# Three small operations per attention unit move from GpSimd to VectorE in six steps of a fused attention and MoE kernel

## The chip, the cores and the metric

One core of a Trainium2 chip runs the kernel. The metric is the device time of one execution in microseconds. Engines are named as in the profile: PE (TensorE; PEld its weight loads), DVE (VectorE), ACT (ScalarE), POOL (GpSimd), SP (SyncE, which issues DMAs).

## The reference

Three layers, one behind the other, all in float32:

```python
def _attn_ref(q, k, v):          # 4 x 8 heads, 576 tokens, head_dim 64
    scores = scale * np.matmul(q, k.transpose(0, 1, 3, 2))
    kth = np.partition(scores, -top_k, axis=-1)[..., -top_k:-top_k + 1]   # top_k = 32
    scores = np.where(scores >= kth, scores, -1000000000.0)
    attn = np.exp(scores - np.max(scores, axis=-1, keepdims=True))
    attn = attn / (np.sum(attn, axis=-1, keepdims=True) + 1e-09)
    return np.matmul(attn, v)

def _moe_ref(x, w_in, w_out):    # x: 2304 x 512, w_in: 512 x 2048, w_out: 2048 x 512
    h = x @ w_in
    g = h * np.clip(h + 3.0, 0.0, 6.0) / 6.0
    return g @ w_out
```

The third layer routes each token to one of 8 experts (512 x 1024 and 1024 x 512) and scales the expert's output by a gate.

## The kernel before, in words

The attention is cut into 72 units, of 128 query rows of two heads each (or the same amount of remaining rows). A loop of 76 steps runs them as a software pipeline: in step i the scores of unit i are made, unit i-1 is searched for its 32 largest scores, unit i-2 is masked, unit i-3 is exponentiated and divided by its sum, unit i-4 is transposed, and every second step two units are multiplied with the values. Between these a step does one eighth of a group of the second layer (`s10`, `s11`, `gate`, `swish`, `large`, `small`, `s20`, `s21`), and up to step 18 it prepares that layer's weights, two pieces a step (`one`, `two`, `round`, `add`, `hi`, `low`, `store`). The routed experts follow from about 700 us on.

The order of the work is written out by hand: the string `FIRST` for steps 0 to 11, `MID` for steps 12 to 20 (`MOES` is 12, `WORDS` 21), `THEN` and `ODD` after that. Each word of the string issues one part, and the engines execute their instructions in that order; there is no other scheduler. What the change and the prediction speak of:

- `pick0` to `pick3` (L474, L477; DVE): four rounds of the search, two MAX8 each, the first three followed by match-and-replace; the last pair has 576 elements a row. `A` holds the 32 values.
- `bounds` (L482, L484; POOL): `nb`, from the largest and the 32nd value, the bias of the exponential and of the mask; and `viol`, differences of the selected values that are looked at once at the end, as a guard on the selection. Both are 128x4.
- `bend` (L488; ACT) and `mask` (L492; POOL): the mask of the next step, from `nb`.
- `expo` (L498; ACT): exponential with the sum of each row in `sums` (128x2).
- `guard` (L502; POOL): adds 1e-9 to `sums`. `inverse` (L505; DVE): reciprocal of it. `scale` (L512 on ACT for units below 16, L514 on POOL after that): multiplies the unit with it.
- `turn` (L525; PE): transposes of the scaled unit, in the next step, and `keep` (L530; ACT), their copy out of PSUM.
- `pairs` (L455 to L459; DVE): five operations that order the scores of the newest unit for the search. `swish` (L619; DVE), `xl` (L575; DVE, behind ACT's `xh`, L560), `small` (L626; POOL, behind ACT's `large`, L623).
- The weights: `one` (L241), `two` (L248) on DVE, `round` (L256) and `hi` (L269) on ACT, `add` (L261, behind `two` and `round`) and `low` (L273, behind `hi`) on POOL. There are 32 pieces; steps 12 to 16 do `one` and `two` for two each, step 17 for the last one.

In `MID` DVE's order is `one0 two0 pick0 one1 pick1 two1 pick2 inverse swish pick3 xl pairs`, and POOL's is `lows low0 guard low1 add0 mask0 add1 mask1 bounds small`.

Of the kernel before, what the change touches and what calls it, by code (L numbers as in the profile page):

```python
# [14 lines left out]
ALU = mybir.AluOpType  # L15
# [8 lines left out]
TOPK = 32  # L24
# [18 lines left out]
RAMP, MOES, WORDS = 3, 12, 21  # L43
FIRST = ("hi0 s10 expo0 lows hi1 turn0 one0 s11 s20 low0 round0 two0 ship keep0 turn1 expo1 guard bend0 keep1 add0 turn2 load0 "
         "store0 one1 load_k inverse keep2 prep mask0 pick0 round1 score0 gate take0 scale two1 bend1 load_q swish large values xh "
         "score1 pick1 pick2 aside s21 add1 load1 xl pick3 need_v low1 take1 store1 pairs mask1 bounds small")
MID = ("lows turn0 hi0 turn1 low0 s10 s11 ship keep0 one0 keep1 expo0 two0 pick0 load_k turn2 store0 one1 pick1 expo1 hi1 guard "
       "round0 bend0 two1 score0 pick2 keep2 low1 s20 take0 gate bend1 inverse add0 score1 values take1 round1 scale swish mask0 "
       "large s21 add1 xh pick3 need_v prep xl mask1 load_q bounds small store1 load0 load1 pairs aside")
THEN = ("lows pick0 turn0 expo0 keep0 ship expo1 pick1 bend0 s10 guard turn1 place pick2 inverse score0 mask0 turn2 s11 take0 "  # L50
        "keep1 bend1 pick3 need_v gate load_k score1 swish keep2 scale aside load_q bounds values take1 mask1 xh large xl prep "
# [47 lines left out]
def layers(tc: tile.TileContext, qt, kt, v, w_in, w_out, embt, tau, w1, w2, out, y_dram, yq_dram, g_dram, tbl, xq_dram, lo_dram, flag, pools, consts):  # L99
    nc = tc.nc  # L100
# [20 lines left out]
    viol = const.tile([128, NUNIT, 2, 2], BF16, name="viol")  # L121
    kb = const.tile([128, 2, 2], F32, name="kb")
# [187 lines left out]
    sel, pts, sums = {}, {}, {}  # L310
# [168 lines left out]
    def bounds(i):  # L479

        A, nb = sel[i]
        nc.gpsimd.tensor_tensor(nb, A[:, :, 0:TOPK:TOPK - 1], kb, op=ALU.mult)  # L482
        if not exact:
            nc.gpsimd.tensor_tensor(viol[:, i, :, :], A[:, :, TOPK - 1:TOPK].broadcast_to([128, 2, 2]), A[:, :, 15:24:8], op=ALU.subtract)  # L484

    def relu(i, n):

# [11 lines left out]

    def guard(i):  # L500
        sel.pop(i)
        nc.gpsimd.tensor_scalar(sums[i], sums[i], 1e-9, None, op0=ALU.add)  # L502

    def inverse(i):
        nc.vector.reciprocal(sums[i], sums[i])  # L505
# [375 lines left out]
    def step(i, last):  # L881
# [15 lines left out]
        def after(o):  # L897
            if last:
# [3 lines left out]
                   s10=lambda: part(a, 1, 0), s11=lambda: part(a, 1, 1), gate=lambda: lows() if i in (1, 2) else part(a, 2), swish=lambda: part(a, 3), large=lambda: part(a, 4), small=lambda: part(a, 5),  # L902
                   s20=lambda: after(0), s21=lambda: after(1), aside=aside, place=place,
                   guard=lambda: at_(3, guard), inverse=lambda: at_(3, inverse), scale=lambda: at_(3, scale), bounds=lambda: at_(1, bounds),
                   pairs=lambda: at_(0, pairs), values=lambda: both(values), xh=lambda: both(finish), xl=lambda: both(finish_low))
        for name, j, f, n in (("bend", 2, relu, 2), ("mask", 2, mask, 2), ("expo", 3, expo, 2), ("pick", 1, select, 4),
# [3 lines left out]
        def pair(f, j, c):  # L910
            n = pair_of(i - j, c)
            if n >= 0:
                f(n)
        for name, f, j in (("load", w_load, -1), ("one", w_one, 0), ("two", w_two, 0), ("round", w_round, 0), ("add", w_add, 0),
                           ("hi", w_hi, 1), ("low", w_low, 1), ("store", w_store, 1)):
            for c in range(2):
                ops[name + str(c)] = lambda f=f, j=j, c=c: pair(f, j, c)
        names = (FIRST if i < MOES else MID if i < WORDS else ODD if i % 2 else THEN).split()
        if i == 0:
# [480 lines left out]
```

## Time and profile before

| | |
|---|---|
| three runs | 1007.87, 1010.01, 1005.36 us (median 1007.87) |
| the profiled execution, its own time | 1007.83 us |
| its span, first to last instruction | 1005.8 us |
| mean granted clock of PE, share of full speed | 0.969 |
| busy share of the span | PE 93%, DVE 77%, ACT 71%, POOL 63% |

In the profile a group or an instruction stands as line, engine, operation, output<-inputs, output<-input (partitions x elements, type) and its count; the time that an engine was idle before an instruction stands in brackets with what ended it. Times in the trace are microseconds from the start of the span. Steps are told apart by `bounds`, which each step issues once: step 12 ends at about 121, step 13 at 131.5, step 14 at 142, step 15 at 153.3, step 16 at 164.7, step 17 at 175.6.

### The profile page before, as it was taken

The numbers are of one execution on the slowest core, as the hardware profiler recorded it, in microseconds if no ns is written. First come the engines' busy times: TensorE is split into PE (matmuls) and PEld (weight loads), VectorE is DVE, ScalarE is ACT, GpSimd is POOL, SyncE is SP. The second block draws the span as 40 slices with busy tenths as digits, with TensorE's granted clock in tenths as the row PEclk, the third lists the DMA queues.
The fourth block names the chain that finished last, engine by engine and source line by source line (L and its number), as shares of the span: only waits on it lengthen the run. The fifth ranks groups of instructions, "written<-read, shape, count | busy, mean of one in ns | idle before, by whom it ended". The sixth has DMA issues, their size and how long they took to land. (4 is left out here: it accounts for less than half of the span.)

```text
span 1005.8 us, 20687 instructions
## 1 busy us (share of the span) xinstructions
PE 934.8 (93%) x7128; PEld 820.3 (82%) x7128; DVE 778.1 (77%) x2364; ACT 712.8 (71%) x1441; POOL 637.9 (63%) x786
## 2 busy tenths in 40 slices
PE   3656688999999999999999999999999999999997
PEld 1433467989899899998998988889898988999986
DVE  7999999899989989989989899882134354666660
ACT  5899889888889788789778787785335454555551
POOL 5889899677778788688788666665333453134210
PEclk9966799999999999999999999999999999999998
DMA  7655676664456754456665476477586467767730
GB/s 251 211 177 162 213 237 234 207 202 149 141 168 195 249 184 131 137 189 192 221 177 146 143 227 202 139 237 203 172 262 223 133 226 263 242 200 239 255 124 23
DMA packets 100689, 193.21 MB, mean 192 GB/s; under 512 B 16189, under 2 KB 42448, under 8 KB 100575
## 3 DMA queue, kind: packets, MB, share of 16 engines
q1 hardware_dynamic: 95983, 181.74, 56.3%
q0 software_dynamic: 4448, 10.00, 3.2%
q8 instruction: 58, 0.95, 0.4%
q14 instruction: 56, 0.46, 0.1%
q10 hardware_dynamic: 144, 0.07, 0.0%
HBM read 163.64 MB, written 24.92 MB: 187 GB/s over the span
## 5 line engine op out<-in xcount | busy, mean ns | idle before, releaser
L492 POOL TENSOR_TENSOR s<-s,z 128x576 f32<-128x576 f32 x144 | 191.4, 1330 | 61.6 <-ACT z L488 61.0
L607 PE MATMUL bank_h<-xh,vh 128*128 128x256 f32 x576 | 171.6, 298 | 0.0
L607 PE MATMUL bank_h<-xh,lo 128*128 128x256 f32 x576 | 163.7, 284 | 0.0
L607 PE MATMUL bank_h<-xl,vh 128*128 128x256 f32 x576 | 163.6, 284 | 0.0
L474 DVE MAX8 A<-left 128x8 f32<-128x288 f32 (+1 forms) x288 | 159.5, 594 | 0.0
L525 PE MATMUL bank_t<-both,s 128*128 128x128 f32 x648 | 108.1, 290 | 30.8 <-ACT pt L530 18.1
L525 PEld LDWEIGHTS bank_t<-both,s 128*128 128x128 f32 x648 | 81.2, 148 | 53.2 <-ACT pt L530 24.2
L530 ACT COPY pt<-bank_t 128x384 f32<-128x384 f32 x216 | 101.5, 478 | 26.2 <-PE bank_t L525 26.2
L626 POOL TENSOR_TENSOR gl<-u,gh 128x512 fp32r<-128x512 f32 x72 | 93.1, 1293 | 41.6 <-ACT gh L623 41.5
L642 PE MATMUL y<-wh,gh 128*128 128x512 f32 x288 | 116.5, 405 | 0.0
L488 ACT ACTIVATE z<-s,nb 128x576 bf16<-128x576 f32 x144 | 112.2, 780 | 4.4 <-POOL nb L482 4.3
L446 ACT COPY s<-ps_sc 128x576 f32<-128x576 f32 x143 | 92.3, 645 | 32.5 <-PE ps_sc L439 11.0
L498 ACT ACTIVATE s<-s,nb 128x576 f32<-128x576 f32 x144 | 113.0, 786 | 1.5 <-POOL s L492 1.5
L642 PE MATMUL y<-lo,gh 128*128 128x512 f32 x288 | 113.5, 394 | 0.0
L642 PE MATMUL y<-wh,gl 128*128 128x512 f32 x288 | 113.2, 393 | 0.0
L607 PEld LDWEIGHTS bank_h<-xl,vh 128*128 128x128 f32 x576 | 111.2, 193 | 0.3
L607 PEld LDWEIGHTS bank_h<-xh,vh 128*128 128x128 f32 x576 | 111.1, 193 | 0.3
L607 PEld LDWEIGHTS bank_h<-xh,lo 128*128 128x128 f32 x576 | 110.7, 192 | 0.0
L1038 POOL DMA_INDIRECT out_dram<-ob,idt x21 | 25.8, 1228 | 123.4 <-ACT ob L1031 92.3
L514 POOL TENSOR_SCALAR s<-s,sums 128x576 f32<-128x576 f32 x112 | 82.5, 748 | 20.7 <-DVE sums L505 20.2
L543 PE MATMUL bank_a<-pt,vt 128*64 128x128 f32 (+1 forms) x1600 | 93.7, 275 | 0.9 <-ACT pt L530 0.9
L615 ACT ACTIVATE u<-bank_h,half 128x512 f32<-128x512 f32 x72 | 50.0, 694 | 61.8 <-PE bank_h L607 61.8
(266 smaller groups left out, 2611.6 us busy)
## 6 DMA issues: line engine op xcount, KB each, us to landing
lo<-lo_dram SPq DMA_DIRECT2D x144, 512.0 KB, 4.6
a<-in_moe_w_dram SPq DMA_DIRECT2D x64, 512.0 KB, 6.1
vt<-in_v_dram SPq DMA_DIRECT2D x28, 320.0 KB, 4.4
w<-in_moe_w_in_dram SPq DMA_DIRECT2D x16, 512.0 KB, 3.9
w<-in_moe_w_out_dram SPq DMA_DIRECT2D x16, 512.0 KB, 4.3
lo_dram<-wf SPq DMA_DIRECT2D x32, 256.0 KB, 2.7
qraw<-in_q_dram SPq DMA_DIRECT2D x48, 128.0 KB, 2.9
krs<-in_k_dram SPq DMA_DIRECT2D x16, 288.0 KB, 4.7
```

Source lines behind the costliest of these rows:

```text
L446: nc.scalar.copy(sbuf[i % NS][:, :, HS * g:HS * g + HS], ps_[i][:, :, :HS])
L474: nc.vector.max(A[:, n, 8 * r:8 * r + 8], src[:, n, :w])
L488: nc.scalar.activation(zb_[n], tile_of(i, n), AF.Relu, bias=sel[i][1][:, n, 1:2], scale=-BIG)
L492: nc.gpsimd.tensor_tensor(s, s, zb_[n], op=ALU.subtract)
L498: nc.scalar.activation(s, s, AF.Exp, bias=sel[i][1][:, n, 0:1], scale=SCALE, accum_out=sums[i][:, n:n + 1])
L514: nc.gpsimd.tensor_scalar(x, x, rv[:, n:n + 1], 1.0, op0=ALU.mult, op1=ALU.mult)
L525: nc.tensor.transpose(pp[:, 128 * k:128 * k + 128], e[:, 128 * (3 * c + k):128 * (3 * c + k) + 128], ident)
L530: nc.scalar.copy(pts[i][:, 3 * c:3 * c + 3, :].rearrange("p k n -> p (k n)"), tb_.pop((i, c))[:, :384])
L543: nc.tensor.matmul(av[64 * n:64 * n + 64, c0:c1], vt[:, k, 64 * n:64 * n + 64], pt[:, k + 5 * n if k < 4 else 4, c0:c1], start=(o == 0), s ...
L607: nc.tensor.matmul(ph[:, a, :], w, x[:, k, :], start=(k == 0 and n == 0), stop=(k == 3 and n == 2))
L626: nc.gpsimd.tensor_tensor(state[q][1], state.pop((q, "u")).rearrange("p (a n) -> p a n", a=2), state[q][0].bitcast(F32), op=ALU.subtract)
L642: nc.tensor.matmul(state["y"][o], x[:, a, c], w, start=(f == 0 and n == 0), stop=(f == 15 and n == 2))
```

## The change

In steps 12 to 17 (`MOES <= step < WORDS - 3`) the two operations of `bounds` and the one of `guard` are issued to DVE instead of POOL; the units are those that are in the respective stage in these steps, six for each stage. In `MID` the word `guard` moves from behind `hi1` to just ahead of `inverse`. Elsewhere the three stay on POOL. Nothing else changes: the operations, their shapes and their data are the same.

```diff
-MID = ("... pick1 expo1 hi1 guard "
-       "round0 bend0 two1 score0 pick2 keep2 low1 s20 take0 gate bend1 inverse add0 score1 ..."
+MID = ("... pick1 expo1 hi1 "
+       "round0 bend0 two1 score0 pick2 keep2 low1 s20 take0 gate bend1 guard inverse add0 score1 ..."
...
     def bounds(i):
         A, nb = sel[i]
-        nc.gpsimd.tensor_tensor(nb, A[:, :, 0:TOPK:TOPK - 1], kb, op=ALU.mult)
+        by = nc.vector if MOES <= i + 1 < WORDS - 3 else nc.gpsimd
+        by.tensor_tensor(nb, A[:, :, 0:TOPK:TOPK - 1], kb, op=ALU.mult)
         if not exact:
-            nc.gpsimd.tensor_tensor(viol[:, i, :, :], A[:, :, TOPK - 1:TOPK].broadcast_to([128, 2, 2]), A[:, :, 15:24:8], op=ALU.subtract)
+            by.tensor_tensor(viol[:, i, :, :], A[:, :, TOPK - 1:TOPK].broadcast_to([128, 2, 2]), A[:, :, 15:24:8], op=ALU.subtract)
...
     def guard(i):
         sel.pop(i)
-        nc.gpsimd.tensor_scalar(sums[i], sums[i], 1e-9, None, op0=ALU.add)
+        (nc.vector if MOES <= i + 3 < WORDS - 3 else nc.gpsimd).tensor_scalar(sums[i], sums[i], 1e-9, None, op0=ALU.add)
```

## Rows read from the trace of the kernel before

**Rows 1.** The page, its first part: busy time, share of the span, instructions.
```profile
PE 934.8 (93%) x7128; PEld 820.3 (82%) x7128; DVE 778.1 (77%) x2364; ACT 712.8 (71%) x1441; POOL 637.9 (63%) x786
```
**Rows 2.** Windows of single steps: length, busy time by engine, granted clock, DMA share, GB/s.
```profile
142.00:153.30 11.30, 11.30 (x93) 9.33 (x92) 11.14 (x31) 10.15 (x21) 11.14 (x12) 0.92 0.70 239
153.30:164.70 11.40, 8.95 (x59) 7.49 (x58) 10.99 (x34) 10.44 (x23) 11.13 (x13) 0.98 0.77 265
164.70:175.60 10.90, 10.55 (x86) 9.49 (x86) 9.88 (x30) 10.90 (x24) 10.73 (x12) 0.86 0.54 168
175.60:184.10 8.50, 8.46 (x58) 7.45 (x57) 8.30 (x30) 8.50 (x18) 7.74 (x10) 1.00 0.52 145
```
**Rows 3.** Waits from 110 to 182 us: total us, times, longest.
```profile
PEld bank_t L525 <- ACT s L512: 11.4, 4, 5.4
...
ACT s L512 <- DVE sums L505: 5.3, 5, 2.5
...
DVE xl L575 <- ACT xh L560: 1.9, 3, 0.9
```
**Rows 4.** Timeline of PE, 160 to 215 us: start, duration, instruction, idle before.
```profile
163.52 1.33 PE L525 MATMUL bank_t<-both,s 128*128 128x128 f32 x6 [1.90 <-ACT s L512]
...
176.14 0.82 PE L525 MATMUL bank_t<-both,s 128*128 128x128 f32 x6
```
**Rows 5.** Timeline of DVE, steps 12 to 14.
```profile
118.48 0.15 DVE L505 RECIPROCAL sums<-sums 128x2 f32<-128x2 f32 x1
...
129.10 0.15 DVE L505 RECIPROCAL sums<-sums 128x2 f32<-128x2 f32 x1
...
133.74 0.42 DVE L241 TENSOR_SCALAR wf<-w 128x512 int32<-128x512 int32 x1
134.19 0.69 DVE L248 SCALAR_TENSOR_TENSOR wf<-w,wf 128x512 int32<-128x512 int32 x1
...
139.79 0.15 DVE L505 RECIPROCAL sums<-sums 128x2 f32<-128x2 f32 x1
139.86 0.66 DVE L619 SCALAR_TENSOR_TENSOR u<-u,bank_h 128x512 f32<-128x512 f32 x1
```
**Rows 6.** Groups by line, DVE, 110 to 176: busy us, mean ns, idle before.
```profile
L248 DVE SCALAR_TENSOR_TENSOR wf<-w,wf 128x512 int32<-128x512 int32 x11 | 11.2, 1021 | 0.2
...
L241 DVE TENSOR_SCALAR wf<-w 128x512 int32<-128x512 int32 x11 | 7.2, 658 | 0.0
```
**Rows 7.** Timeline of DVE at 215 and at 704 us.
```profile
215.56 0.70 DVE L182 TENSOR_SCALAR nr<-nr,tb 128x8 f32<-128x8 f32 x1
...
704.98 0.35 DVE L755 TENSOR_TENSOR pos<-pos,picks 128x16 f32<-128x16 f32 x1
```
**Rows 8.** Timeline of POOL at the same places.
```profile
215.50 0.73 POOL L415 TENSOR_TENSOR ql<-qraw,qh 128x256 fp32r<-128x256 f32 x1 [0.69 <-ACT qh L408]
...
704.01 1.28 POOL L626 TENSOR_TENSOR gl<-u,gh 128x512 fp32r<-128x512 f32 x1 [4.37 <-ACT gh L623]
```
**Rows 9.** Timeline of POOL, steps 12 to 14.
```profile
118.44 1.28 POOL L492 TENSOR_TENSOR s<-s,z 128x576 f32<-128x576 f32 x1
...
129.01 1.29 POOL L261 TENSOR_TENSOR wf<-wf,w 128x512 int32<-128x512 int32 x1 [0.27 <-ACT w L256]
...
134.41 0.54 POOL L502 TENSOR_SCALAR sums<-sums 128x2 f32<-128x2 f32 x1 [1.31 <-ACT s L498]
...
139.42 1.29 POOL L261 TENSOR_TENSOR wf<-wf,w 128x512 int32<-128x512 int32 x1
```
**Rows 10.** Groups by line, POOL, 110 to 176 us.
```profile
L502 POOL TENSOR_SCALAR sums<-sums 128x2 f32<-128x2 f32 x6 | 2.0, 342 | 1.7 <-ACT s L498 1.3
...
L482 POOL TENSOR_TENSOR nb<-A,kb 128x4 f32<-128x4 f32 x6 | 1.2, 200 | 0.9 <-DVE A L474 0.9
```
**Rows 11.** Timeline of DVE at 347 us, each reading what the one before wrote.
```profile
347.65 0.17 DVE L736 TENSOR_REDUCE mxs<-l_all 128x4 f32<-128x32 f32 x1
347.86 0.19 DVE L738 TENSOR_TENSOR eqs<-l_all,mxs 128x32 f32<-128x32 f32 x1
```

More of the change, by code (lines that the diff above doesn't have):

```diff
@@ L46 @@
          "score1 pick1 pick2 aside s21 add1 load1 xl pick3 need_v low1 take1 store1 pairs mask1 bounds small")
-MID = ("lows turn0 hi0 turn1 low0 s10 s11 ship keep0 one0 keep1 expo0 two0 pick0 load_k turn2 store0 one1 pick1 expo1 hi1 guard "
-       "round0 bend0 two1 score0 pick2 keep2 low1 s20 take0 gate bend1 inverse add0 score1 values take1 round1 scale swish mask0 "
+MID = ("lows turn0 hi0 turn1 low0 s10 s11 ship keep0 one0 keep1 expo0 two0 pick0 load_k turn2 store0 one1 pick1 expo1 hi1 "
+       "round0 bend0 two1 score0 pick2 keep2 low1 s20 take0 gate bend1 guard inverse add0 score1 values take1 round1 scale swish mask0 "
        "large s21 add1 xh pick3 need_v prep xl mask1 load_q bounds small store1 load0 load1 pairs aside")
```

## The prediction

> **What bounds the kernel now.** I began with the page: over the span TensorE (PE) is busiest, 934.8 us of 1005.8 [rows 1]. That is an average over stages, and the change touches only steps 12 to 17 of the attention loop, 110 to 176 us, so I read the windows of single steps next [rows 2]. In step 14 to 15 (142.0 to 153.3) VectorE (DVE) is busy 11.14 of 11.30 us and GpSimd (POOL) also 11.14; one step on, 10.99 and 11.13 of 11.40, with PE at 8.95. In step 17 to 18 (175.6 to 184.1) PE has 8.46 of 8.50 and POOL falls to 7.74. So two engines are full in the steps that are changed, and PE is full right behind them. Which of the two full ones sets the pace is read from who waits [rows 3]: PE's weight loads waited 11.4 us for ACT's scaling L512, ACT's scaling waited 5.3 us for DVE's inverse L505, DVE itself waited only 1.9 us, for an ACT copy. In this stretch nobody's row names POOL's bounds, differences or guards as what it waited for. The chain is: DVE's queue, inverse, ACT's scale, PE's transposes of the next step. PE last waits on it at 163.52 (1.90 us idle behind L512); the transposes of the step after, at 176.14, start with no wait [rows 4]. So what DVE loses up to the inverse of step 16 goes to the end one for one; what it loses after that meets a PE that is behind anyway.
>
> **What DVE's time holds.** An unhindered L241 took 0.42 us and L248 0.69 (at 133.74 and 134.19) [rows 5]; over steps 12 to 17 the eleven of each have means of 0.658 and 1.021 us [rows 6]. That is 11 x 0.24 + 11 x 0.33 = 6.2 us in which DVE executes nothing but is not idle in the record. What it waits for shows best in two small operations. A TENSOR_SCALAR of 128x8 took 0.70 us, from 215.56 to 216.26, and a TENSOR_TENSOR of 128x16 with both inputs in SBUF 0.35 us, from 704.98 to 705.33 [rows 7]; POOL was inside an operation both times, from 215.50 to 216.23 and from 704.01 to 705.29 [rows 8]. Both ended some 0.03 to 0.04 us behind POOL. The inverse, a reciprocal with one input, took its 0.15 us at 118.48, 129.10 and 139.79 [rows 5] although POOL was inside L492 or L261 each time [rows 9]. So some forms on DVE wait until POOL's running operation is over, and the three that the change brings are of the two forms that waited: the guard is a TENSOR_SCALAR, bounds and differences are TENSOR_TENSORs with two SBUF inputs.
>
> **The change part by part.**
>
> *Leaving POOL.* Per step POOL loses a guard (0.34 us), bounds (0.20) and differences (as long as the bounds) [rows 10]: 0.74 us. I cost this at nothing, since nobody waits for POOL there; if that cover is gone it is a gain, the first rival. No operation that moves issues a DMA, so no queue of SP or POOL changes its order. In steps 18 to 20 the guard stays on POOL and is only written further down the list; on POOL's queue it passes nothing there (the second weight subtraction is empty by then): nothing.
>
> *Issue time on DVE.* Independent small operations start 0.07 us apart (139.79 and 139.86) [rows 5], one that needs the result of the one before 0.21 (347.65 and 347.86) [rows 11]. The inverse needs the guard: 0.21. The bounds need the last MAX8: 0.14 over the usual step of 0.07; the differences 0.07. That is 0.21 for the guard and 0.21 for the pair. The guard itself waits for nothing new: the POOL guard that began at 134.41 had ACT's exponential [rows 9], 5 us ahead of the inverse at 139.79. Five guards (steps 12 to 16) and four pairs (steps 12 to 15) lie ahead of PE's last wait: 5 x 0.21 + 4 x 0.21 = 1.9 us.
>
> *The guard's wait for POOL.* It stands where the inverse starts now, so what POOL still had to run at that moment is the price. Step 12: L492 from 118.44 for 1.28, inverse at 118.48, 1.24 us left. Step 13: L261 from 129.01 for 1.29, 129.10, 1.20 left. Step 14: 139.42 plus 1.29 less 139.79, 0.92 left [rows 5, 9]; steps 15 and 16 repeat this with 0.92 and 0.89. It is no accident: L261 needs the L248 that DVE ran some 1.6 us before, so POOL is inside L261 or the L492 behind it. Bounds: nothing, and 5 x 1.29 = 6.5. In step 12 POOL was ahead by 0.04 us only, so I take half of it: 0.62 + 1.20 + 0.92 + 0.92 + 0.89 = 4.55 us. Queued behind the guard are inverse, gating product, last MAX8 pair, pairs; ACT's scale waits for the inverse, PE for that.
>
> *The bounds' wait for POOL.* Once POOL no longer holds its own bounds it goes from L492 straight to the subtraction L626 (1.28 us, the one at 704.01 [rows 8]) or to the next weight subtraction. The pair reaches DVE about when that starts. Bounds: nothing, and one whole operation, 4 x 1.28 = 5.1 us. Neither end is nearer; half, 2.6 us, or 0.64 per step. Behind the pair are the five pair operations and the next step's weight words; ACT wants the bounds only a few us later.
>
> On who goes first when both want it, the trace has only one DVE operation at a time waiting. The Trainium skill ("SBUF — State Buffer", section "Who interferes with whom") says that the first to issue has the shared pair for the whole instruction and the other is blocked fully. The two small operations of this trace agree (0.70 and 0.35 us); by that rule POOL, waiting while the bounds run, would go ahead of the differences in every step, and the sum would hold 5.1 us in place of 2.6.
>
> *The old collisions.* The 6.2 us of L241 and L248 can shrink or grow once everything shifts. POOL keeps all its long operations and loses 0.74 of some 11 us, so I take no change; ends: all gone (-6.2), and a quarter more (+1.5).
>
> *Steps 16 (bounds) and 17.* Covered by PE's full queue from 164.7 on (10.55 of 10.90 us) [rows 2]: nothing; without that cover two pairs and one guard, some 3 us.
>
> **Sum.** 1.9 + 4.55 + 2.6 = 9.05 us. The profiled execution took 1007.83 us with a span of 1005.8; the median of the three runs is 1007.87, so both bases agree: **1016.9 us**.
>
> **Rivals.**
>
> 1. *POOL is the pace, and it becomes shorter: faster.* For it: POOL is as full as DVE [rows 2], and DVE's fullness holds 6.2 us of waiting. Against: no wait names POOL's bounds. If each of the six steps shrinks by the 0.74 us, and the six together by POOL's idle time ahead of guards and bounds (1.7 + 0.9 us) [rows 10], that is 4.4 + 2.6 = 7.0 us: 1000.8 us. It decides if DVE's operations lose their long forms in steps 12 to 16. Chance 0.11.
> 2. *The guard doesn't wait, the pair does.* The TENSOR_SCALAR that waited had 8 elements and a scalar read from memory; the guard has 2 and a constant. Then 1.9 + 2.6 = 4.5 us: 1012.3 us. Chance 0.17.
> 3. *None waits.* 1.9 us: 1009.7 us, and down to 1003.5 if the old collisions go too. For it stands only the small size of the operations. Chance 0.13.
> 4. *Every pair pays a whole POOL operation*, the differences behind the bounds: 1.9 + 4.55 + 5.1 = 11.55 us: 1019.4 us. POOL takes its turn in a gap as short as that between two DVE operations. Chance 0.12.
>
> By the rule of the Trainium skill named above this fourth case would be the outcome; the trace of before has no two such DVE operations in a row to show it.
>
> **How the numbers follow.** My forecast has 0.47. Its own range is 1011.5 to 1020.0 (4.55 down to 1, or 5.2 and 5.1 in full). About 0.5% of the time, 5 us, is what a measurement can tell from no change: 1002.8 to 1012.9. Faster is the first rival alone, 0.11. Slower is the forecast (0.47) without its low end (0.05), the fourth (0.12) and about a third of the second (0.06): 0.60. The rest, 0.29, is the same. For 8 in 10 the range runs from the third rival's low end, 1003.5, to 1021.5 (the fourth with a collision or two more); outside lie the first rival and some 0.07 above.
>
> **What would show it.** In the changed kernel's timeline of steps 12 to 16 the guard on DVE should last 0.8 to 1.3 us and end with a POOL L261 or L492; an inverse should follow 0.2 us behind it. Of the two small TENSOR_TENSORs behind the fourth MAX8 pair at least one in most steps should last over 0.5 us. Steps 12 to 16 should take about 2 us more each, PE's waits for L512 should grow by the same sum, and everything from 182 us on should be the old course, later by about 9 us. If the guards last 0.2 us, my largest term is gone. If the step is not longer although they wait, DVE was not the pace. If L241 and L248 become short, the old collisions paid for the new.

## The result and the profile after

The changed kernel takes 1014.85 us (median of 6 runs, 1013.33 to 1015.62), the kernel before 1007.06 on the same chip. The medians lie 7.8 us apart; the ratio taken over the single runs is 1.0071, with a 95% interval of 1.0058 to 1.0085. It is slower by 7 to 8 us. The forecast was 1016.9, in a range of 1003.5 to 1021.5.

The page of the changed kernel, first part, against [rows 1]: the span grew by 8.1 us, from 1005.8 to 1013.9; DVE has 7.4 us more, POOL 5.2 less, PE the same work.

```profile
PE 936.1 (92%) x7128; PEld 821.7 (81%) x7128; DVE 785.5 (77%) x2382; ACT 712.3 (70%) x1441; POOL 632.7 (62%) x768
```

Windows of the steps that answer to [rows 2], cut where the step's bounds are done, columns as there. By this cut step 15 (the first line) grew by 2.3 us, step 16 by 1.4 and step 17 by 1.7. In step 16 DVE alone is full: of 12.80 us PE has 7.67 and POOL 8.45, which was full before.

```profile
145.00:158.60 13.60, 13.60 (x102) 11.65 (x101) 12.76 (x38) 12.28 (x27) 11.87 (x10) 0.83 0.67 228
158.60:171.40 12.80, 7.67 (x48) 6.74 (x47) 12.66 (x35) 8.48 (x17) 8.45 (x7) 0.95 0.52 175
171.40:184.00 12.60, 12.00 (x100) 10.75 (x99) 12.03 (x36) 11.88 (x26) 11.46 (x9) 0.92 0.56 184
184.00:192.00 8.00, 7.60 (x49) 6.16 (x48) 7.97 (x30) 8.00 (x17) 6.20 (x8) 1.00 0.48 134
```

The waits, from 110 to 190 us in place of 110 to 182 (L513 and L506 are the L512 and L505 of before, one line further down), against [rows 3]: PE's weight loads wait 17.1 us for the scaling where it was 11.4, the scaling 10.9 us for the inverse where it was 5.3. POOL now waits for others.

```profile
PEld bank_t L526 <- ACT s L513: 17.1, 3, 7.0
PE bank_t L526 <- ACT s L513: 15.7, 3, 6.6
ACT s L513 <- DVE sums L506: 10.9, 4, 4.3
POOL gl L627 <- ACT gh L624: 6.9, 4, 2.3
...
DVE xl L576 <- ACT xh L561: 1.9, 3, 0.7
```

PE's timeline, against [rows 4]: the last wait for the scaling is now at 170.21 (163.52 before) and is 5.12 us long (1.90). The first line is step 12.

```profile
120.83 1.54 PE L526 MATMUL bank_t<-both,s 128*128 128x128 f32 x6 [6.56 <-ACT s L513]
...
170.21 1.54 PE L526 MATMUL bank_t<-both,s 128*128 128x128 f32 x6 [5.12 <-ACT s L513]
```

DVE's timeline, the guards of steps 12 to 16 with an inverse behind the third: three last 0.98 to 1.25 us, two 0.15.

```profile
118.46 1.25 DVE L503 TENSOR_SCALAR sums<-sums 128x2 f32<-128x2 f32 x1
...
130.19 0.15 DVE L503 TENSOR_SCALAR sums<-sums 128x2 f32<-128x2 f32 x1
...
141.66 0.98 DVE L503 TENSOR_SCALAR sums<-sums 128x2 f32<-128x2 f32 x1
142.68 0.17 DVE L506 RECIPROCAL sums<-sums 128x2 f32<-128x2 f32 x1
...
153.82 0.15 DVE L503 TENSOR_SCALAR sums<-sums 128x2 f32<-128x2 f32 x1
...
167.92 1.17 DVE L503 TENSOR_SCALAR sums<-sums 128x2 f32<-128x2 f32 x1
```

POOL's timeline at the same moments. The guard of 118.46 ends at 119.71 and POOL's L493 (the mask, L492 before) at 118.41 + 1.28 = 119.69; that of 141.66 ends at 142.64, L261 at 142.62; that of 167.92 at 169.09, L493 at 169.06. In steps 13 and 15 POOL's L261 began only at 130.94 and 154.74, since it waited for ACT's L256: at 130.19 and 153.82 POOL executed nothing, and the guard passed.

```profile
118.41 1.28 POOL L493 TENSOR_TENSOR s<-s,z 128x576 f32<-128x576 f32 x1
...
130.94 1.30 POOL L261 TENSOR_TENSOR wf<-wf,w 128x512 int32<-128x512 int32 x1 [1.12 <-ACT w L256]
...
141.34 1.28 POOL L261 TENSOR_TENSOR wf<-wf,w 128x512 int32<-128x512 int32 x1
...
154.74 1.30 POOL L261 TENSOR_TENSOR wf<-wf,w 128x512 int32<-128x512 int32 x1 [1.27 <-ACT w L256]
...
167.79 1.27 POOL L493 TENSOR_TENSOR s<-s,z 128x576 f32<-128x576 f32 x1
```

ACT's timeline ahead of the late L261 of step 13: L256 stood behind a copy of the scores, which waited for PE. In the kernel before (second fence) that copy came 1.9 us sooner.

```profile
120.00 1.44 ACT L513 ACTIVATE s<-s,sums 128x576 f32<-128x576 f32 x2 [4.19 <-DVE sums L506]
...
129.63 0.64 ACT L446 COPY s<-ps_sc 128x576 f32<-128x576 f32 x1 [1.56 <-PE ps_sc L435]
130.17 0.70 ACT L256 ACTIVATE w<-w 128x512 int32<-128x512 uint32 x1
```
```profile
118.66 1.44 ACT L512 ACTIVATE s<-s,sums 128x576 f32<-128x576 f32 x2 [2.54 <-DVE sums L505]
...
127.70 0.64 ACT L446 COPY s<-ps_sc 128x576 f32<-128x576 f32 x1 [0.98 <-PE ps_sc L435]
128.24 0.69 ACT L256 ACTIVATE w<-w 128x512 int32<-128x512 uint32 x1
```

DVE's timeline, the pairs of steps 12, 13 and 15 (bounds L483, differences L485), and POOL's at the last: the bounds of step 15 last 1.29 us, for which POOL's L627 runs; the differences never last over 0.16.

```profile
121.89 0.16 DVE L483 TENSOR_TENSOR nb<-A,kb 128x4 f32<-128x4 f32 x1
121.97 0.16 DVE L485 TENSOR_TENSOR viol<-A 128x4 bf16<-128x4 f32 x1
...
132.93 0.58 DVE L483 TENSOR_TENSOR nb<-A,kb 128x4 f32<-128x4 f32 x1
133.43 0.15 DVE L485 TENSOR_TENSOR viol<-A 128x4 bf16<-128x4 f32 x1
...
157.26 1.29 DVE L483 TENSOR_TENSOR nb<-A,kb 128x4 f32<-128x4 f32 x1
158.47 0.15 DVE L485 TENSOR_TENSOR viol<-A 128x4 bf16<-128x4 f32 x1
```

```profile
157.25 1.28 POOL L627 TENSOR_TENSOR gl<-u,gh 128x512 fp32r<-128x512 f32 x1
158.49 0.75 POOL L415 TENSOR_TENSOR ql<-qraw,qh 128x256 fp32r<-128x256 f32 x1
```

**The account.** Between the inverse of step 11 and that of step 16 the changed kernel needs 6.5 us more (59.4 us from 103.13 to 162.51, now 65.9 from 103.25 to 169.12). Every duration on DVE in this stretch is in the trace, so the 6.5 us can be divided: what the guards last beyond 0.14 us each, what the pairs last beyond 0.16 each, what the L241 and L248 last more or less than before, what DVE is idle more (the stretch less DVE's busy time in it), and a rest, which is the added instructions' own time without a wait. The same for every run below, from its own profiled execution (us):

| run | ratio to before, 95% interval | steps 12 to 16 | guards' waits | pairs' waits | L241, L248 | idle | rest |
|---|---|---|---|---|---|---|---|
| the change | 1.0071 (1.0058 to 1.0085) | +6.5 | 3.0 | 1.6 | -0.3 | 0.7 | 1.6 |
| e1, guard only | 1.0060 (1.0038 to 1.0082) | +6.2 | 3.0 | 0 | 1.7 | 0.7 | 0.8 |
| e2, bounds only | 1.0000 (0.9985 to 1.0015) | +0.2 | 0 | 0.9 | -1.5 | 0.1 | 0.8 |
| e3, guard one port | 1.0040 (1.0025 to 1.0055) | +3.2 | 0 | 0.8 | 0 | 0.9 | 1.6 |
| e5, none two ports | 1.0032 (1.0015 to 1.0049) | +3.1 | 0 | 1.1 | -0.2 | 0.7 | 1.6 |
| e6, order only | 1.0011 (1.0002 to 1.0021) | +1.5 | 0 | 0 | 1.4 | 0.1 | -0.1 |
| e7, no guard | 1.0004 (0.9989 to 1.0019) | +2.1 | 0 | 0 | 1.9 | 0.3 | -0.1 |
| e8, guard elsewhere | 1.0054 (1.0037 to 1.0071) | +3.7 | 2.3 | 0.5 | -0.2 | 0.2 | 1.0 |
| e9, the same alone | 1.0045 (1.0029 to 1.0061) | +3.1 | 3.4 | 0 | -0.5 | 0.1 | 0.2 |
| e10, guard as a sum, alone | 1.0027 (1.0008 to 1.0045) | +3.1 | 0 | 0 | 1.7 | 0.6 | 0.8 |
| e11, the same, all units | 1.0092 (1.0066 to 1.0117) | +1.2 | 0 | 0 | -0.4 | 0.7 | 0.9 |

The columns of the account are one execution each, rounded, and end at the inverse of step 16; the ratios are of 6 to 12 runs against 16 to 29 of the kernel before (6 against 6 for the change itself). Counted on to the inverse of step 20, the same executions lost 7.2 us (the change), 6.3 (e1), 0.6 (e2), 3.9 (e3), 3.7 (e5), 1.5 (e6), 2.2 (e7), 5.3 (e8), 3.7 (e9), 3.2 (e10) and 1.8 (e11). That is within 1 us of what the ratios say, but for e7, whose profiled execution was 1.6 us above its median, and e11, which loses most of its time later.

### The profile page after: what moved, and what is told of

It reads as the page before. It is cut to its first block, busy times and chain, and to the rows that moved or that the text cites. A ratio compares the mean times of both kernels' runs of the same rounds, so it can differ in the third digit from the quotient of the medians.

```text
span 1013.9 us, 20690 instructions
## 1 busy us (share of the span) xinstructions
PE 936.1 (92%) x7128; PEld 821.7 (81%) x7128; DVE 785.5 (77%) x2382; ACT 712.3 (70%) x1441; POOL 632.7 (62%) x768
## 5 line engine op out<-in xcount | busy, mean ns | idle before, releaser
L493 POOL TENSOR_TENSOR s<-s,z 128x576 f32<-128x576 f32 x144 | 190.9, 1327 | 62.1 <-ACT z L489 61.6
L627 POOL TENSOR_TENSOR gl<-u,gh 128x512 fp32r<-128x512 f32 x72 | 92.8, 1290 | 48.0 <-ACT gh L624 47.9
```

The lines of the kernel that those rows point to most:

```text
L493: nc.gpsimd.tensor_tensor(s, s, zb_[n], op=ALU.subtract)
L627: nc.gpsimd.tensor_tensor(state[q][1], state.pop((q, "u")).rearrange("p (a n) -> p a n", a=2), state[q][0].bitcast(F32), op=ALU.subtract)
```

## The experiments

**Theory**: guards and bounds on DVE wait until POOL's running operation is over, as their forms do [rows 7, 8], and PE waits for that through inverse and scaling. **Rivals**: any instruction more on DVE costs this; POOL's relief counts; the old weight operations L241 and L248 merely meet POOL otherwise.

**One part alone.** e1 keeps the guard on DVE and puts the bounds back; e2 the opposite, with the old order.

```diff
 # e1
-        by = nc.vector if MOES <= i + 1 < WORDS - 3 else nc.gpsimd
+        by = nc.gpsimd
 # e2, and MID as before
-        (nc.vector if MOES <= i + 3 < WORDS - 3 else nc.gpsimd).tensor_scalar(sums[i], ...)
+        nc.gpsimd.tensor_scalar(sums[i], ...)
```

> Only the guard goes to VectorE, ahead of the inverse; bounds and differences stay on GpSimd. Port theory (VectorE waits for GpSimd's running operation): in the changed kernel the five guards of steps 12 to 16 take 3.9 us from their start to the inverse's, the four pairs 2.2 us; this run keeps the first sum: 3 to 5 us slower than the kernel before. Rival, collisions of the weight operations that merely fall otherwise: guards and pairs are not what counts, and the result is anywhere between 0 and 8 us with guards of 0.15 us. Rival, relief of GpSimd: faster than before.

> Only bounds and differences go to VectorE; the guard stays on GpSimd in its old place. Port theory: 4 pairs, 0.2 us of issue each and one wait of up to 1.3 us in every second step, 2 to 3.5 us slower than before; the differences right behind the bounds never wait (0.15 us each). Rival, collisions: no relation to the pairs' own durations.

Measured: 1.0060 and 1.0000. The guard is most of the change. Both amounts lie beside what was expected, e1 near 6 us where 3 to 5 was, e2 at nothing where 2 to 3.5 was, and the account shows what came on top: guards (3.0) and pairs (0.9) waited as the theory has it, but L241 and L248 lost 1.7 us in e1 and won 1.5 in e2. That they met POOL otherwise is read from the timelines; no run holds it fixed. DVE's timeline of e1 in step 16, where POOL's two L273 ran from 159.86 to 162.61 nearly without a gap: L241 1.58 and L248 1.67 us, which took 0.42 and 0.69 unhindered [rows 5].

```profile
159.87 1.58 DVE L241 TENSOR_SCALAR wf<-w 128x512 int32<-128x512 int32 x1
161.49 1.67 DVE L248 SCALAR_TENSOR_TENSOR wf<-w,wf 128x512 int32<-128x512 int32 x1
...
168.09 1.17 DVE L503 TENSOR_SCALAR sums<-sums 128x2 f32<-128x2 f32 x1
```

**The same place, another form.** e3 is the changed kernel with the guard as a sum over one element; the 1e-9 is left out in these units. In e5, besides, the bounds take their constants from PSUM (four columns of `bank_a` that nothing else uses, filled once).

```diff
 # e3 and e5, for the six units
-            nc.vector.tensor_scalar(sums[i], sums[i], 1e-9, None, op0=ALU.add)
+            nc.vector.tensor_reduce(sums[i], sums[i].unsqueeze(2), axis=AX.X, op=ALU.add)
 # e5
+    kbp = bank_a[:, 0, 252:256].rearrange("p (n k) -> p n k", n=2)
-        by.tensor_tensor(nb, A[:, :, 0:TOPK:TOPK - 1], kb, op=ALU.mult)
+        by.tensor_tensor(nb, A[:, :, 0:TOPK:TOPK - 1], kbp if by is nc.vector else kb, op=ALU.mult)
```

> The changed kernel, with the guard of these six units in a form of one input that takes no second port: a sum over one element (TENSOR_REDUCE), which leaves the 1e-9 out. The number of VectorE instructions is the same. Port theory: this operation lasts 0.15 to 0.2 us in every step, also inside a GpSimd operation, and the run gains back the guards' waits, about 3 us: 3.5 to 5 us slower than before. Rival, issue and dependence on VectorE alone: no gain, 7 to 8 us slower than before.

> As the run with the sum over one element, and the bounds' constants lie in PSUM, so that the bounds have one SBUF input (values unchanged). The differences still have two, but stand right behind. Port theory: guards and bounds of 0.15 to 0.2 us; of the wait the differences may take over up to a part, since they are now the first of the pair with two SBUF inputs: 1.5 us slower than before if they don't wait, up to 4 us if they inherit the bounds' wait. Issue theory: 7 to 8 us slower.

Measured: 1.0040, inside what was expected, its interval below the change's; some 3 us are back, by the form of the guard alone. DVE's group of e3 from 103 to 170 us has the five at a mean of 138 ns, and in step 14 one at 141.14 beside POOL's L261, which began at 140.80.

```profile
L504 DVE TENSOR_REDUCE sums<-sums 128x2 f32<-128x2 f32 x5 | 0.7, 138 | 0.0
```
```profile
141.14 0.14 DVE L504 TENSOR_REDUCE sums<-sums 128x2 f32<-128x2 f32 x1
```
```profile
140.80 1.28 POOL L261 TENSOR_TENSOR wf<-wf,w 128x512 int32<-128x512 int32 x1
```

e5 gave 1.0032, inside what was expected for an inherited wait. DVE's timeline of its step 15, and POOL's: the bounds, with one SBUF input, began 0.01 us behind POOL's L631 and took 0.15 us; the differences, with two, 0.06 us later, took 1.24, until POOL's 154.66 + 1.29 = 155.95.

```profile
154.67 0.15 DVE L484 TENSOR_TENSOR nb<-A,bank_a 128x4 f32<-128x4 f32 x1
154.73 1.24 DVE L486 TENSOR_TENSOR viol<-A 128x4 bf16<-128x4 f32 x1
```
```profile
154.66 1.29 POOL L631 TENSOR_TENSOR gl<-u,gh 128x512 fp32r<-128x512 f32 x1
```

**Order and relief by themselves.** e6 has the new order with all three on POOL; e7 is the kernel before without the guard of the six units, so their 1e-9 is left out; bounds and differences stay on POOL.

```diff
 # e6: MID as in the change, guard and bounds on nc.gpsimd
 # e7, on the kernel before
+        if not MOES <= i + 3 < WORDS - 3:
             nc.gpsimd.tensor_scalar(sums[i], sums[i], 1e-9, None, op0=ALU.add)
```

> Only the order is changed: the guard stands ahead of the inverse in the list, but all three operations stay on GpSimd. Port theory: on GpSimd's queue the guard merely changes places with one weight subtraction, and is done about 2 us ahead of the inverse: no change beyond 1.5 us either way, from collisions of the old weight operations. Rival, the new place itself holds the inverse back: 2 us or more slower, with the inverse waiting for GpSimd in the list of waits.

> The kernel before, with the guard left out for the six units (1e-9 not added); bounds and differences on GpSimd. GpSimd is relieved, VectorE has nothing added. Port theory: nobody waits for GpSimd here, so the relief by itself gains nothing beyond what collisions do, 1.5 us either way. Rival, relief of GpSimd pays: 2 us or more faster.

Measured: 1.0011 and 1.0004. Neither the place in the list nor the relief of POOL from its guards moves the time by more than some 2 us; in e7 POOL has less to do and nothing is faster. What both profiled executions lost, 1.5 and 2.1 us, stands with L241 and L248 (1.4 and 1.9).

**The same form, another place.** e8 puts the changed kernel's guard right behind the step's first L248; e9 does that with the bounds on POOL.

```diff
-MID = ("... expo0 two0 pick0 ... one1 pick1 expo1 hi1 round0 ... bend1 guard inverse ..."
+MID = ("... expo0 expo1 two0 guard pick0 ... one1 pick1 hi1 round0 ... bend1 inverse ..."
```

> The changed kernel, with the guard on VectorE right behind the first weight word pair of the step (L248), where GpSimd mostly waits for that L248, and the second half of the exponential ahead of it in the list (ScalarE's own order is the same). Same operations, same counts. Port theory: guards of 0.15 us, about 3 us won back: 3.5 to 5 us slower than before. Rival, the form of the operation costs wherever it stands: 7 to 8 us slower.

> As the run before, but bounds and differences stay on GpSimd. Port theory: no port wait is left that the change brought; 5 x 0.15 us of issue and collisions of the old weight operations of 2 us either way: between 1 us faster and 3 us slower than before. Rival, collisions always grow with anything on VectorE: 5 us or more slower.

Measured: 1.0054 and 1.0045, both slower than expected. The place was badly chosen: POOL does not wait for L248 there in every step. DVE's timeline of e8 in step 13 shows the guard at 124.05 for 1.25 us, and POOL's an L273 from 123.99 to 125.27. In steps 12, 14 and 16 the same guard took 0.15 to 0.16 us, in step 15 1.24. The wait goes with what POOL executes at that moment, wherever the guard stands; so this miss speaks for the theory, not for its rival. In e8 the guard of step 17 lasted 1.25 us too, and of the loss in that step 1.6 us stayed to step 20, which the account does not hold.

```profile
124.05 1.25 DVE L503 TENSOR_SCALAR sums<-sums 128x2 f32<-128x2 f32 x1
...
173.74 1.25 DVE L503 TENSOR_SCALAR sums<-sums 128x2 f32<-128x2 f32 x1
```
```profile
123.99 1.28 POOL L273 TENSOR_TENSOR wf<-wf,wh 128x512 fp32r<-128x512 f32 x1 [0.86 <-ACT wh L269]
```

**A guard that leaves nothing out.** e10 is e1 with a sum over two elements, the row sum and a stored 1e-9, next to which the exponential writes its sums in all units; e11 has this guard on DVE for all 72 units.

```diff
+    sum_ = [wk.tile([128, 2, 2], F32, name=f"sums{i}") for i in range(4)]
...
-            nc.vector.tensor_scalar(sums[i], sums[i], 1e-9, None, op0=ALU.add)
+            sums[i] = sm.tile([128, 2], F32, tag="sums", name="sums")
+            nc.vector.tensor_reduce(sums[i], sum_[i % 4], axis=AX.X, op=ALU.add)
```

> Bounds and differences on GpSimd; the guard of the six units on VectorE in the very place of the run with the guard only, but as a sum over two elements, the row sum and a stored 1e-9 (TENSOR_REDUCE, one input; nothing is left out). Place, engine and number of operations are those of the run with the guard only, which was 6 us slower than before. Port theory: the operation lasts under 0.2 us also inside a GpSimd operation, 5 x 0.15 to 0.2 us of issue is left, and collisions of up to 2 us: between 0.5 us faster and 2.5 us slower than before. Rival, place and dependence cost: about 6 us slower.

> The same form of guard on VectorE for all 72 units. In the later steps TensorE is full and the guard's way over GpSimd is covered, in the early ones VectorE is full: port theory 0 to 4 us slower than before; rival, one hand-over less between engines pays in 72 steps: 2 us or more faster, a version better than both.

Measured: 1.0027 for e10, where e1 had 1.0060 with the other form in the same place. That is some 2.7 us, just over what was expected, and the account has the excess with L241 and L248 (1.7). The two intervals of the ratio touch, but the accounts agree within 0.1 us in every part save one: the 3.0 us of the guards' waits are the 3.1 us between e1's steps and e10's. DVE's group of e10 for the five:

```profile
L506 DVE TENSOR_REDUCE sums<-sums 128x2 f32<-128x4 f32 x5 | 0.7, 140 | 0.0
```

e11 gave 1.0092, far above what was expected. Only a part is lost in steps 12 to 16: the inverse of step 17 comes 2.0 us late, the 31st of the 72 inverses 4.8 (325.7 against 320.9), the 51st 6.7 (510.9 against 504.2). The waits of e11 from 200 to 700 us show on what:

```profile
DVE sums L506 <- ACT s L500: 41.9, 27, 3.7
...
POOL nb L484 <- DVE A L475: 21.4, 14, 1.5
...
PEld bank_t L531 <- POOL s L520: 4.8, 9, 1.0
```

In the later steps the guard stands ahead of the third round of the search (even steps, `THEN`) or of the fourth (odd steps, `ODD`); in the timeline its waits lie in the odd steps. On POOL it waited for the exponential too (22.3 us in 20 waits before) and nobody was behind it in a hurry; on DVE the search waits behind it (41.9 us in 27 waits), the bounds on POOL wait for the search (21.4 us, 0.8 before), and PE for POOL's scaling, of which the same stretch before has no line. That the placing in those steps is the cause is read from these waits; no run with another placing was made. No version was found that beats the kernel before.

## Why the prediction was right, and where not

- *What bounds.* Right. DVE sets the pace of these steps: of what it lost up to the inverse of step 16 (6.5 us), 5.7 us show as longer waits of PE's weight loads for the scaling, and nothing came back behind. That POOL is as full was no sign of a bound: the change relieved it of all three, left it 8.45 us of work in the 12.80 of step 16, and was slower; e7 relieved it of the guards alone and gained nothing. That is the end of the first rival.
- *The guard's wait.* Right in kind, and about its price where it came: 1.25, 0.98 and 1.17 us in steps 12, 14 and 16, where 1.24, 0.92 and 0.89 were read; in step 12 the whole wait came, of which the sum held half. Missed for steps 13 and 15. The step of the prediction that failed is "so POOL is inside L261 or the L492 behind it": L261 also waits for ACT's L256, as the 0.27 us at 129.01 in [rows 9] showed already, and so it began 0.75 and 0.92 us after the guard (130.94 and 154.74 against 130.19 and 153.82). In step 13 ACT's L256 stood behind a copy that waited 1.56 us for PE's scores (0.98 before); PE had waited 6.56 us for the scaling of step 12 (4.91 before), and that 4.19 us for the inverse (2.54). So one guard's wait let the next one pass. This chain is read from the waits; for step 15 it was not followed so far. 3.0 us instead of 4.55. The second rival, that a guard of two elements doesn't wait, fell with the 1.25 us.
- *The pair.* 1.6 us of waits instead of 2.6 (0.42 in step 13, 1.13 in step 15), all of them on the bounds. The differences waited in no step of the change, so the fourth rival fell; only when e5 took the port from the bounds did the wait pass to them.
- *Issue.* 1.9 us, as forecast: the 1.6 us of the rest, and 0.3 us that the account has as idle time, in the hand-over to the inverse (0.19) and ahead of the bounds (0.08). The other 0.46 us of idle time stand behind ACT's `xh` (1.40 against 0.94): not in the sum.
- *The old collisions.* -0.3 us where 0 was forecast; a lucky zero. Step 13 won 0.5, step 15 0.5, step 16 lost 0.9. Over the runs it goes from -1.5 to +1.9 us, which is the main reason why parts don't add up: e1 misses its range by it, e2 most of the way, in opposite directions.
- *Step 17 and after.* Forecast as free. The inverse of step 17 was 7.94 us late, where that of step 16 was 6.6; by step 20 it is 7.3, and that stays to the end of the loop. So 0.7 us got through, and the rest of the 8.1 us of span, of one execution each, came behind the loop. In e3 and e5 0.6 to 0.7 us got through, in e1 and e10, where the pair stays on POOL, under 0.1; in e8 and e9, whose guard of step 17 lasted 1.25 and 1.27 us, 1.6 and 0.5. The cover was there, but not whole.

Together 6.5 + 0.7 against 9.05: both waits were sized by the moment at which they would meet POOL, and the change itself moved these moments. That the total came so near is in part luck: two guards that waited for nothing are partly set off by the whole wait of step 12, the idle time behind `xh` and step 17. The low end of the forecast's own range, 1011.5, does not follow from its working: with 1 us in place of 4.55 the sum gives 1013.3.

## What to carry to other kernels

An instruction that is moved to a full engine costs its issue time and what its form waits for: look for the same form at the same size elsewhere in the trace, next to an operation of the other engine, before calling it small. Here 0.15 us of work took up to 1.25 us, as long as POOL's running operation still had to go, and the same sum written in a one-input form took 0.14, though e10 as a whole stayed 2.7 us slower than leaving the guard on POOL. A full engine for which nobody waits is no reason to unload it.

## What the runs showed of the hardware

- A TENSOR_SCALAR of 128x2 with a constant waits for a running POOL operation (1.25, 0.98 and 1.17 us in the change, 0.15 where POOL had nothing); a TENSOR_REDUCE over the row sums in its place does not (0.14 us in all five steps of e3, of e5 and of e10; in ten of these fifteen POOL was inside an operation). A TENSOR_TENSOR with both inputs in SBUF waits (up to 1.29 us), with one of them in PSUM it does not (0.15 to 0.16 us in e5). It goes the other way too: in the kernel before, POOL's own guard at 134.41 took 0.54 us, up to just behind DVE's L248 (134.19 and 0.69 us) [rows 5, 9], and 0.21 us at 170.32.
- The second of two such operations in a row did not wait again: in the change the differences, 0.08 us behind bounds that ran freely or right behind bounds that had waited, took 0.15 to 0.16 us each time. POOL's next operation, L415 at 158.49, took 0.75 us, where its form took 0.74 on the mean from 100 to 300 us. The Trainium skill ("SBUF — State Buffer", section "Who interferes with whom") lets the first to issue have the pair of ports; the trace agrees for each operation alone, and does not show POOL coming between two of DVE's that stand together.
- Over these runs, each a small edit, L241 and L248 alone moved the steps by -1.5 to +1.9 us, by how they met POOL. Most parts of 1 to 3 us could only be told apart by the account by instructions beside the ratio.
